# One tuned kernel, four edits: layer-norm scale as multiply then add, a first chunk without DMA transposes, reordered denominator matmuls, refitted planner constants

## The chip, the cores and the metric

The kernel runs on one NeuronCore of a Trainium2 chip. Time is device microseconds (us) of one execution. Kernels that are compared ran in turn on the same chip. A run has one number more, the granted clock: the mean share of full speed at which TensorE was allowed to run.

## The reference, cut to what matters

Two kinds of layer alternate, four layers in all, on x of 2048 positions by 512 features (bf16).

```python
def _A_ref(x, wqkv, wo):      # local: each position sees 8 positions, two apart; 32 heads of 16
    ...
    logits = jnp.where(mask[None, None, :, :], logits, -1e9)
    attn = _softmax(logits, axis=-1)
    ...
def _B_ref(x, wq, wk, wv, wo):    # full attention, 32 query heads, one shared key and value head
    ...
    p = _softmax(scores, axis=-1)
    ...
x = A_x
x = x + _A_ref(_layernorm(x, axis=-1), A_wqkv, A_wo)
x = x + _B_ref(_layernorm(x, axis=-1), B_wq, B_wk, B_wv, B_wo)
x = x + _A_ref(_layernorm(x, axis=-1), A_wqkv, A_wo)
x = x + _B_ref(_layernorm(x, axis=-1), B_wq, B_wk, B_wv, B_wo)
```

Full attention needs 32 x 2048 x 2048 exponentials per layer, twice. That is most of the work.

## The kernel before

The program is laid out by a **planner** in Python, when the kernel is built. Each operation has an estimated duration and a list of engines that may do it. The planner plays the run through in its own time and emits the instructions of every engine in the order of the played start times. Each engine is given this fixed order and waits at semaphores. An estimate that is off changes no result, but it can put an instruction that must wait ahead of one that could run.

The sequence is cut into four chunks of 512 positions. A chunk goes through layer norm, q/k/v, local attention, output, second layer norm, and the projections of full attention. A stream of tiles (128 keys by 512 queries) of full attention runs beside this, each tile's exponentials on ScalarE ("pt") or on VectorE with GpSimd ("t", "i"). The first pair of layers must have all four chunks before it can do most of its tiles.

```python
MM, SWITCH, DMA = 216.0, 90.0, 620.0                       # planned durations, ns
LAT = {"pe": 264.0, "act": 170.0, "dve": 135.0, "pool": 120.0, "sp": 2400.0}
BIAS = {"act": 0.0, "act2": 150.0, "vec": 120.0, "pv": 200.0, "copy": 0.0, "pass": 140.0}
...
def ln(self, src, deps, after=(0.0,) * 4):                 # layer norm of one chunk, four tiles
    ...                                                    # statistics on VectorE, power on GpSimd
    for i in range(4):
        def norm(op, i=i, xn=xn):
            self.chain(op.eng, self.pick(op).tensor_scalar(
                out=xn.t[:], in0=src(i), scalar1=mv[:, i, 0:1], scalar2=rstd[:, i:i + 1],
                op0=ALU.subtract, op1=ALU.mult))
        n = ... self.op({"dve": 690.0, "pool": 900.0}, 0, norm, [pw, *xn.prev], ...)
        tr = self.op("sp", 1250.0, ... nc.sync.dma_start_transpose(
                out=xnT[:, :, i * 128:(i + 1) * 128], in_=xn.t[:]) ...)
...
def split(op):                                             # K of a chunk into its masked layout
    for g in range(4):
        for h in range(2):
            r = slice(32 * g + 16 * h, 32 * g + 16 * h + 16)
            self.chain("sp", nc.sync.dma_start(out=self.k.t[r, :, :, h, :], in_=...))
...
ms = self.op("dve", 400.0, mask, [ex], ...)                # mask of the local probabilities
...
for j in range(2):                                         # denominators, by column half j
    ...
    runs = [(dj, pj[:, :, SPILL:NQ]), (dj[:, b0:4, 0:SPILL], pj[:, b0:4, 0:SPILL])]
    for out, rhs in runs:
        self.chain("pe", nc.tensor.matmul(out, lhsT=self.w.halves[:, gh, :], rhs=rhs, ...,
                                          tile_position=(0, 64 * j)))
```

## Time and profile before

| | kernel before |
|---|---|
| time | 1702.98 us, median of 3 (1702.31 to 1707.58) |
| span of the profiled run, granted clock | 1703.6 us, 0.916 |
| busy share: TensorE, VectorE, ScalarE, GpSimd | 92, 86, 83, 55% |
| first exponential of full attention | 87.7 us |

A busy share is an average over stages with different limits. The prediction below therefore reads it by stage. Lines of the profile name instructions by line, engine and tiles: `PE o L1289` is a matmul that writes tile `o`, issued by line 1289.

### The profile page before, as it was taken

Reading aid. Unit: us, or ns where it says so; the run is one execution under the profiler, and the core shown is the slowest. Engines: PE = TensorE matmul, PEld = TensorE weight load, DVE = VectorE, ACT = ScalarE, POOL = GpSimd, SP = SyncE. Lnnn points to the kernel's source line nnn. Section 1 sums busy time; section 2 is a strip of 40 time slices with the busy share of each in tenths; the row PEclk is TensorE's granted clock in tenths of the full one; section 3 lists DMA queues with packets and bytes.
Section 4 is the critical chain, followed back from the end, with each engine's and each line's share of the span. In section 5 each row is a group of like instructions: output and inputs, shape, how many; then the busy total and the mean of one; then the engine's idle time right before and its main releaser. Section 6 shows DMA issues by size and latency. Waiting matters only on the chain.

```text
span 1703.6 us, 41207 instructions
## 1 busy us (share of the span) xinstructions
PE 1559.3 (92%) x16604; PEld 522.1 (31%) x16643; DVE 1458.8 (86%) x2466; ACT 1416.0 (83%) x1718; POOL 943.0 (55%) x702
## 2 busy tenths in 40 slices
PE   3698989899999999999999999899999999999996
PEld 1343433422332224322342223322222222222221
DVE  2567685899789996899779997799999999999996
ACT  2375867698879987899878997699999999998994
POOL 4425354546465654666455663555666656565664
PEclk9577978799979997999979999799999999999997
DMA  5010101001100001000110001000100000000000
GB/s 149 15 26 14 27 11 29 6 14 37 31 21 12 11 22 26 14 14 12 22 23 17 12 18 26 3 17 4 38 24 12 12 24 11 13 13 23 12 18 14
DMA packets 101262, 36.02 MB, mean 21 GB/s; under 512 B 88840, under 2 KB 94600, under 8 KB 101064
## 3 DMA queue, kind: packets, MB, share of 16 engines
q1 hardware_dynamic: 100200, 31.48, 8.7%
q8 instruction: 132, 2.16, 0.5%
q10 hardware_dynamic: 864, 1.84, 0.3%
q14 instruction: 66, 0.54, 0.1%
HBM read 13.53 MB, written 2.61 MB: 9 GB/s over the span
## 4 chain that ended last, share of the span: by engine, by line
PE 38%; DVE 35%; ACT 15%; issue 8%; POOL 2%; DMA 1%; SPq 1%; DVEq 0%; ACTq 0%; POOLq 0%
DVE t L1268 24%; ACT pt L1264 14%; PE o L1289 12%; PE st L1249 8%; DVE i L1277 3%; PE y L992 3%; PE dv L1249 3%; PE oa L1171 2%; PE oa L1159 2%; PE q L992 2%; PE k L992 2%; PE qb L992 2%; DVE xn L1023 1%; PE v L1085 1%; PE st L1134 1%
## 5 line engine op out<-in xcount | busy, mean ns | idle before, releaser
L1264 ACT ACTIVATE pt<-st 128x1024 bf16<-128x1024 f32 x1306 | 1221.9, 1073 | 124.8 <-PE o L1289 55.4
L1273 POOL TENSOR_TENSOR i<-t,off 128x1024 int32<-128x1024 int32 x372 | 703.0, 1890 | 580.7 <-DVE i L1277 317.0
L1268 DVE TENSOR_SCALAR t<-dv 128x512 int16<-128x512 f32 x1485 | 931.7, 681 | 101.7 <-PE dv L1249 96.3
L1289 PE MATMUL o<-i,VEd 128*32 128x512 f16 x1470 | 280.8, 409 | 4.9 <-POOL i L1273 3.7
L1289 PE MATMUL o<-i,region 128*32 128x512 f16 x1500 | 277.2, 394 | 3.1 <-DVE i L1277 2.3
L1249 PE MATMUL dv<-QT,KAB 32*128 32x512 bf16 x735 | 264.0, 399 | 17.2 <-DVE t L1268 14.8
L1277 DVE TENSOR_SCALAR i<-t 128x2048 int16<-128x2048 int16 x372 | 267.0, 719 | 14.7 <-PE o L1289 6.3
L1249 PE MATMUL st<-QT,KAB 32*128 32x512 bf16 x1313 | 262.1, 400 | 15.4 <-ACT pt L1264 12.0
L1249 PE MATMUL dv<-QT,region 32*128 32x512 bf16 x750 | 262.0, 387 | 7.2 <-DVE t L1268 4.8
L1249 PE MATMUL st<-QT,region 32*128 32x512 bf16 x1298 | 255.1, 389 | 14.7 <-ACT pt L1264 11.4
L1289 PE MATMUL o<-pt,VEa 128*32 128x512 bf16 x1313 | 248.8, 413 | 2.5 <-DVE t L1268 0.6
L1289 PE MATMUL o<-pt,region 128*32 128x512 bf16 x1298 | 247.3, 397 | 0.0
L1289 PE MATMUL o<-t,VEd 128*32 128x512 f16 x735 | 195.2, 414 | 0.0
L1289 PE MATMUL o<-t,region 128*32 128x512 f16 x750 | 190.2, 394 | 1.0 <-DVE t L1268 1.0
L1249 PEld LDWEIGHTS <-KAB 32*128 32x128 bf16 x2048 | 87.0, 92 | 263.3 <-issue 256.4
L1249 PEld LDWEIGHTS <-region 32*128 32x128 bf16 x2048 | 84.1, 91 | 266.5 <-issue 262.2
L1289 PEld LDWEIGHTS <-region 128*32 128x32 f16 (+1 forms) x3548 | 82.1, 95 | 190.8 <-issue 179.1
L1289 PEld LDWEIGHTS <-VEd 128*32 128x32 f16 x2205 | 77.4, 96 | 129.0 <-issue 121.0
L1140 ACT ACTIVATE P<-st 128x576 bf16<-128x576 f32 (+1 forms) x128 | 80.3, 651 | 22.8 <-PE st L1134 22.1
L1146 DVE TENSOR_TENSOR P<-P,bandmask 128x288 int32<-128x288 int32 x128 | 71.2, 589 | 32.6 <-ACT P L1140 32.3
L1196 POOL TENSOR_TENSOR logs<-logs 128x256 f32<-128x256 f32 x64 | 41.9, 655 | 78.9 <-ACT rec L1187 78.8
L1289 PEld LDWEIGHTS <-VEa 128*32 128x32 bf16 x1313 | 57.6, 96 | 75.8 <-issue 70.8
(127 smaller groups left out, 1190.9 us busy)
## 6 DMA issues: line engine op xcount, KB each, us to landing
lb<-rd SPq DMA_DIRECT2D x31, 256.0 KB
k<-oncA SPq DMA_DIRECT2D x64, 64.0 KB
X<-X SPq DMA_DIRECT2D x124, 32.0 KB
w_sb<-in_A_wqkv_dram ACTq DMA_DIRECT2D x4, 384.0 KB
region<-in_A_x_dram SPq DMA_DIRECT2D x3, 512.0 KB
out_dram<-w_sb SPq DMA_DIRECT2D x3, 512.0 KB
xnT<-xn SPq DMA_TRANSPOSE x64
S<-X SPq DMA_DIRECT2D x62, 8.0 KB
```

The costliest lines, as they stand in the source:

```text
L992: self.chain("pe", self.nc.tensor.matmul(ps[:], lhsT=lhsT, rhs=rhs, start=(n == 0), stop=(n == len(pairs) - 1)))
L1140: ex = self.op("act", act_ns(2 * ncol), lambda op, P=P, sc=sc: self.chain("act", nc.scalar.activation(out=P.t[:, :, c0:UC], in_=self.st.po ...
L1146: self.chain(op.eng, self.pick(op).tensor_tensor(out=x, in0=x, in1=self.w.band[:].unsqueeze(1).to_broadcast([128, 8, NQ // 2]), op=ALU.bit ...
L1159: self.chain("pe", nc.tensor.matmul(o[32 * r:32 * r + 32, 0, q0:q0 + w], lhsT=vv[64 * a:64 * a + 64, j, 16 * gh:16 * gh + 32], rhs=P.t[64 ...
L1171: self.chain("pe", nc.tensor.matmul(out, lhsT=self.w.halves[:, gh, :], rhs=rhs, start=False, stop=False, skip_group_check=True, tile_posit ...
L1196: self.chain("pool", nc.gpsimd.tensor_tensor(out=lg.t[:], in0=lg.t[:], in1=lg.t[:], op=ALU.mult))
L1249: self.chain("pe", self.nc.tensor.matmul(out, lhsT=self.KAB[l][32 * g:32 * g + 32, a, kt * 128:(kt + 1) * 128], rhs=self.QT[32 * g:32 * g ...
L1264: self.chain("act", self.nc.scalar.activation(out=self.pt[pt][:, 0:n, :], in_=self.st.pop(key)[:, 0:n, :], func=AF.Exp, scale=E_SCALE))
L1268: self.chain("dve", self.nc.vector.tensor_scalar(out=self.t[buf][:, r, :].bitcast(I16), in0=self.dv[bank][:], scalar1=-U_BIAS, scalar2=U_B ...
L1273: i = self.nc.gpsimd.tensor_tensor(out=self.i[out][:, 0:n, :].bitcast(I32), in0=self.t[buf][:, 0:n, :].bitcast(I32), in1=self.w.off2[:, 0: ...
L1277: i = self.nc.vector.tensor_scalar(out=self.i[out][:, 0:n, :].bitcast(I16), in0=self.t[buf][:, 0:n, :].bitcast(I16), scalar1=J_OFF[j], sca ...
L1289: self.chain("pe", self.nc.tensor.matmul(self.o[bank][32 * g:32 * g + 32, :], lhsT=lhsT, rhs=rhs, start=first, stop=last, tile_position=(0 ...
```

## The change

Its intent: shorten the serial start (no DMA transposes, no DMA for K in the first chunk), let ScalarE take part of the layer norm, let the denominator matmuls of the two column halves overlap, and give the planner durations closer to the chip's.

```diff
-MM, SWITCH, DMA = 216.0, 90.0, 620.0
-LAT = {"pe": 264.0, "act": 170.0, "dve": 135.0, "pool": 120.0, "sp": 2400.0}
+MM, SWITCH, DMA = 216.0, 101.0, 620.0
+LAT = {"pe": 264.0, "act": 180.0, "dve": 142.0, "pool": 120.0, "sp": 2400.0}
... (evictions 41 and 19 ns shorter, exponentials 8 shorter, copies 605 -> 599, statistics 620 -> 596)
-    BIAS = {"act": 0.0, "act2": 150.0, "vec": 120.0, ...
+    BIAS = {"act": 0.0, "act2": 150.0, "vec": 180.0, ...
...
+        nm = ... nc.vector.scalar_tensor_tensor(out=nmr, in0=mv[:, :, 0], scalar=-1.0, in1=rstd,
+                                                op0=ALU.mult, op1=ALU.mult)
...
+                if op.eng == "act":
+                    k = nc.scalar.activation(out=xn.t[:], in_=src(i), func=AF.Identity,
+                                             scale=rstd[:, i:i + 1], bias=nmr[:, i:i + 1])
+                else:
+                    k = self.pick(op).tensor_scalar(..., scalar1=rstd[:, i:i + 1],
+                                                    scalar2=nmr[:, i:i + 1], op0=ALU.mult, op1=ALU.add)
...
+            if quick:                                       # chunk 0 of the first pair only
+                ... nc.tensor.transpose(out=pT[:, ft, :], in_=xn.t[:, ft * 128:(ft + 1) * 128], ...)
+                ... copy of pT into xnT on ScalarE or VectorE
...
+            if quick:
+                e0 = self.evac(m, self.k.t[:, t, :, 0, :], ..., self.w.kmask[:, 0:1])
+                e1 = self.evac(m, self.k.t[:, t, :, 1, :], ..., self.w.kmask[:, 1:2])
...
-            ms = self.op("dve", 400.0, mask, [ex], ...)
+            ms = self.op("dve", 500.0, mask, [ex], ...)
...
-                for j in range(2):          # both runs of half 0, then both of half 1
+                for q0, q1, b1 in ((SPILL, NQ, 0), (0, SPILL, b0)):
+                    for j in range(2):      # the wide run of both halves, then the narrow one
```

More of the change, by code (lines that the diff above doesn't have):

```diff
@@ L434, in act_ns @@
 def act_ns(cols, pointers=0):
-    return 93.0 + 0.833 * cols + 93.0 * pointers
+    return 52.0 + 0.833 * cols + 93.0 * pointers
 def dve_ns(cols):
-    return 85.0 + 1.04 * cols
+    return 66.0 + 1.04 * cols
 class Op:
@@ L583 @@
     GROUP = 4
-    BIAS = {"act": 0.0, "act2": 150.0, "vec": 120.0, "pv": 200.0, "copy": 0.0, "pass": 140.0}
+    BIAS = {"act": 0.0, "act2": 150.0, "vec": 180.0, "pv": 200.0, "copy": 0.0, "pass": 140.0}
     def __init__(self, sched, segments, ready, io):
@@ L688, in exp @@
         n = len(tiles)
-        t = 426.7 * n + 60
+        t = 426.7 * n + 52
         S.run("act", s, t)
@@ L709, in copy @@
         r, buf = len(self.filling), self.group_buf
-        done = s + 605 + LAT["dve"]
+        done = s + 599 + LAT["dve"]
         self.filling.append((tl, done))
-        S.run("dve", s, 605.0)
+        S.run("dve", s, 599.0)
         S.give(("bank", "vec"), bank, done)
@@ L716, in copy @@
         if len(self.filling) == self.GROUP:
-            self.flush(s + 605, None)
+            self.flush(s + 599, None)
     def flush(self, s, _):
@@ L730, in do_pass @@
         n = len(tiles)
-        t = 133.5 * n + 72 if e == "dve" else POOL_COL * 256 * n + 110
+        t = 134.0 * n + 70 if e == "dve" else POOL_COL * 256 * n + 110
         S.run(e, s, t)
@@ L995, in mm_full, with ln @@
         return self.op("pe", len(pairs) * MM, emit, deps, want=("bank", "aux"), solid=True, prio=self.PRIO, after=after)
-    def ln(self, src, deps, after=(0.0,) * 4):
+    def ln(self, src, deps, after=(0.0,) * 4, quick=False):
         nc = self.nc
@@ L1000, in ln @@
         stats, mv = sm.t[:, :, 0:6], sm.t[:, :, 6:8]
-        ve, rstd = (sm.t[:, :, n] for n in (8, 9))
+        ve, rstd, nmr = (sm.t[:, :, n] for n in (8, 9, 10))
         st = []
@@ L1005, in emit @@
                 self.chain("dve", nc.vector.bn_stats(out=stats[:, i, :], in_=src(i)))
-            st.append(sm.used(self.op("dve", 620.0, emit, [*deps[i], *sm.prev], prio=self.PRIO, after=after[i])))
+            st.append(sm.used(self.op("dve", 596.0, emit, [*deps[i], *sm.prev], prio=self.PRIO, after=after[i])))
         def aggr(op):
@@ L1016, in ln @@
             out=rstd, in0=ve, in1=self.w.nhalf[:], op=ALU.pow)), [ag], prio=self.PRIO))
+        nm = sm.used(self.op("dve", 250.0, lambda op: self.chain("dve", nc.vector.scalar_tensor_tensor(
+            out=nmr, in0=mv[:, :, 0], scalar=-1.0, in1=rstd, op0=ALU.mult, op1=ALU.mult)), [pw], prio=self.PRIO))
         self.xnT.renew()
@@ L1022, in norm @@
             def norm(op, i=i, xn=xn):
-                self.chain(op.eng, self.pick(op).tensor_scalar(
-                    out=xn.t[:], in0=src(i), scalar1=mv[:, i, 0:1], scalar2=rstd[:, i:i + 1], op0=ALU.subtract,
-                    op1=ALU.mult))
-            n = xn.used(sm.used(self.op({"dve": 690.0, "pool": 900.0}, 0, norm, [pw, *xn.prev], prio=self.PRIO,
-                                        port=("pool",))))
-            tr = self.op("sp", 1250.0, lambda op, i=i, xn=xn: self.chain("sp", nc.sync.dma_start_transpose(
-                out=xnT[:, :, i * 128:(i + 1) * 128], in_=xn.t[:])), [n, *self.xnT.prev], prio=self.PRIO)
@@ L1031, in ln @@
-            done.append(self.xnT.used(xn.used(tr)))
+                if op.eng == "act":
+                    k = nc.scalar.activation(out=xn.t[:], in_=src(i), func=AF.Identity, scale=rstd[:, i:i + 1],
+                                             bias=nmr[:, i:i + 1])
+                else:
+                    k = self.pick(op).tensor_scalar(out=xn.t[:], in0=src(i), scalar1=rstd[:, i:i + 1],
+                                                    scalar2=nmr[:, i:i + 1], op0=ALU.mult, op1=ALU.add)
@@ new lines, in norm, with turn @@
+                self.chain(op.eng, k)
+            n = xn.used(sm.used(self.op({"act": 830.0, "dve": 690.0, "pool": 940.0}, 0, norm, [nm, *xn.prev],
+                                        prio=self.PRIO, port=("pool",))))
+            cols = xnT[:, :, i * 128:(i + 1) * 128]
+            if quick:
+                def turn(op, xn=xn):
+                    pT = self.psum(op, [128, 4, 128], BF16, "pT")
+                    for ft in range(4):
+                        self.chain("pe", nc.tensor.transpose(out=pT[:, ft, :], in_=xn.t[:, ft * 128:(ft + 1) * 128],
+                                                             identity=self.w.ident[:]))
+                tr = xn.used(self.op("pe", 400.0, turn, [n, *self.xnT.prev], want=("bank", "aux"), solid=True,
+                                     prio=self.PRIO))
+                tr = self.op({"act": act_ns(512), "dve": 400.0}, 0, lambda op, cols=cols, tr=tr: self.chain(
+                    op.eng, (nc.scalar.copy if op.eng == "act" else nc.vector.tensor_copy)(
+                        out=cols, in_=self.y.pop(tr)[:])), [tr], frees=[tr], prio=self.PRIO)
+            else:
+                tr = xn.used(self.op("sp", 1300.0, lambda op, cols=cols, xn=xn: self.chain(
+                    "sp", nc.sync.dma_start_transpose(out=cols, in_=xn.t[:])), [n, *self.xnT.prev], prio=self.PRIO))
@@ L1032, in ln @@
+            done.append(self.xnT.used(tr))
         return done
@@ L1043, in chunk @@
         after = ((7300.0, 7300.0, 8800.0, 8800.0) if c == 0 else (9000.0 + 2500.0 * c,) * 4) if first else (0.0,) * 4
-        xops = self.ln(src, deps, after)
-        qkv = self.qkv(c, xops)
+        xops = self.ln(src, deps, after, l == 0 and c == 0)
+        qkv = self.qkv(c, xops, l == 0 and c == 0)
         units = [self.unit(c, t, kd, qkv) for kd in range(2) for t in range(4)]
@@ L1049, in chunk, with qkv @@
         return adds
-    def qkv(self, c, xops):
+    def qkv(self, c, xops, quick):
         nc, w_sb = self.nc, self.w.w_sb
@@ L1063, in qkv @@
             m = self.proj(lambda kt: w_sb[:, kt, D + t * 128:D + (t + 1) * 128], xops + self.oncA.prev, "k")
+            if quick:
+                view = lambda m=m: self.y[m][:].rearrange("p (b i) -> p b i", i=64)
+                e0 = self.evac(m, self.k.t[:, t, :, 0, :], view, 512, (), False, self.w.kmask[:, 0:1])
+                e1 = self.evac(m, self.k.t[:, t, :, 1, :], view, 512, [e0], True, self.w.kmask[:, 1:2])
+                kp.append([self.k.used(e0), self.k.used(e1)])
+                continue
             kp.append(self.oncA.used(self.evac(m, self.oncA.t[:, t, :], lambda m=m: self.y.pop(m)[:], 512)))
@@ L1072, in split @@
                         in_=self.oncA.t[r].rearrange("p t (b i) -> p t b i", i=64)))
-        k = [self.k.used(self.oncA.used(self.op("sp", 8 * DMA, split, [*kp, *self.k.prev], prio=self.PRIO)))] * 4
+        k = kp if quick else [[self.k.used(self.oncA.used(self.op("sp", 8 * DMA, split, [*kp, *self.k.prev],
+                                                                  prio=self.PRIO)))]] * 4
         vb = self.v.renew()
@@ L1100, in keep @@
                                                          in_=vb.t[:, 7, :, :, 2 * DH:VW]))
-            self.spill = self.op("pool", 1600.0, keep, [k[0], *v, *self.ks.prev, *self.vs.prev],
+            self.spill = self.op("pool", 1600.0, keep, [*k[0], *(k[3] if quick else ()), *v, *self.ks.prev, *self.vs.prev],
                                  port=("pool",))
@@ L1136, in score @@
                             stop=True, tile_position=(32 * g, 0), skip_group_check=True))
-            sc = self.op("pe", 300.0, score, [*qo[t], ko[t], *extra, *P.prev], want=("slot", "exp"),
+            sc = self.op("pe", 300.0, score, [*qo[t], *ko[t], *extra, *P.prev], want=("slot", "exp"),
                          solid=True, mode="row", prio=self.PRIO)
@@ L1147, in mask @@
                     out=x, in0=x, in1=self.w.band[:].unsqueeze(1).to_broadcast([128, 8, NQ // 2]), op=ALU.bitwise_and))
-            ms = self.op("dve", 400.0, mask, [ex], prio=self.PRIO, port=("dve",))
+            ms = self.op("dve", 500.0, mask, [ex], prio=self.PRIO, port=("dve",))
             def pv(op, gh=gh, P=P):
@@ L1163, in pv @@
                             begun.add(r)
-                for j in range(2):
-                    dj = o[64 * j:64 * j + 64, 1, :]
-                    dj = dj.rearrange("p (b q) -> p b q", q=64)
-                    pj = P.t[:, j, :].rearrange("p (b q) -> p b q", q=NQ)
-                    b0 = 0 if over else 1
-                    runs = [(dj, pj[:, :, SPILL:NQ]), (dj[:, b0:4, 0:SPILL], pj[:, b0:4, 0:SPILL])]
-                    for out, rhs in runs:
-                        self.chain("pe", nc.tensor.matmul(out, lhsT=self.w.halves[:, gh, :], rhs=rhs, start=False,
-                                                          stop=False, skip_group_check=True, tile_position=(0, 64 * j)))
+                b0 = 0 if over else 1
+                for q0, q1, b1 in ((SPILL, NQ, 0), (0, SPILL, b0)):
+                    for j in range(2):
+                        self.chain("pe", nc.tensor.matmul(
+                            o[64 * j:64 * j + 64, 1, :].rearrange("p (b q) -> p b q", q=64)[:, b1:4, 0:q1 - q0],
+                            lhsT=self.w.halves[:, gh, :],
+                            rhs=P.t[:, j, :].rearrange("p (b q) -> p b q", q=NQ)[:, b1:4, q0:q1],
+                            start=False, stop=False, skip_group_check=True, tile_position=(0, 64 * j)))
             kw = dict(want=("bank", "aux")) if gh == 0 else {}
-            m = self.op("pe", 310.0 + SWITCH + 190.0, pv, [ms, *vo, *extra, *pvs], solid=True, mode="c64",
+            m = self.op("pe", 340.0 + SWITCH + 150.0, pv, [ms, *vo, *extra, *pvs], solid=True, mode="c64",
                         prio=self.PRIO - 100.0, **kw)
@@ L1218, in b_in @@
         cs = slice(c * 512, (c + 1) * 512)
-        xops = self.ln(lambda i: self.x_sb[:, 4 * c + i, :], [[a] for a in adds])
+        xops = self.ln(lambda i: self.x_sb[:, 4 * c + i, :], [[a] for a in adds], quick=l == 0 and c == 0)
         done = []
@@ L1306, in evac @@
                        nc.vector.tensor_tensor(out=X.t[:], in0=X.t[:], in1=o[:], op=ALU.add))
-        e = X.used(self.op("dve", 605.0, evac, X.prev if fresh else list(X.cur), after=when, frees=[held], prio=-300.0))
+        e = X.used(self.op("dve", 599.0, evac, X.prev if fresh else list(X.cur), after=when, frees=[held], prio=-300.0))
         if self.parts_left[block]:
@@ L1377, in out_rows @@
                                          for t in range(4)], [self.ready[l, qc, t] for t in range(4)], "y"))
-        return self.op("dve", 605.0, lambda op: self.add_y(l, qc, qi, self.y.pop(m)[:]), [m], frees=[m], prio=-100.0)
+        return self.op("dve", 599.0, lambda op: self.add_y(l, qc, qi, self.y.pop(m)[:]), [m], frees=[m], prio=-100.0)
     def retire_w(self):
@@ L1437, in close_tail @@
         re = log.used(rec.used(self.op("act", act_ns(512), recip, [ln, *rec.prev])))
-        on = rec.used(self.op("dve", 605.0, scale, [re, self.retired]))
+        on = rec.used(self.op("dve", 599.0, scale, [re, self.retired]))
         rec.used(self.op("pool", 3000.0, see, [on, self.wiped]))
@@ L1465, in close_tail @@
             m = self.op("pe", MM, end, [on, begun[qi // 2]], solid=True)
-            self.op("dve", 605.0, lambda op, qi=qi: self.add_y(l, qc, qi, y[qi]), [m])
+            self.op("dve", 599.0, lambda op, qi=qi: self.add_y(l, qc, qi, y[qi]), [m])
     def run(self):
```

## The prediction

> **What bounds the kernel now.** I read the page's busy row and its 40 slices first, then busy time by stage, then the chain of waits over the first 120 us, then single groups of instructions.
>
> The slices say where the slack is. Nothing is full in the first two slices (0 to 85 us). In slices 3 to 8 (85 to 340 us) TensorE is full by the digits while VectorE and ScalarE hover between 5 and 8. From slice 9 to the last all three are close to full, and there the exponentials of the big attention, split between ScalarE and VectorE, are the work that counts.
>
> ```profile
> PE   3698989899999999999999999899999999999996
> DVE  2567685899789996899779997799999999999996
> ACT  2375867698879987899878997699999999998994
> PEclk9577978799979997999979999799999999999997
> ```
>
> By stage, over the last full-rate stretch (1107 to 1618 us, 511 us), the sums are PE 491, DVE 498, ACT 486: 96, 97 and 95%. No change of order can gain much there. The start is another matter. The columns are stretch, length, then busy us of PE, PEld, DVE, ACT, POOL, then the granted clock, DMA share and GB/s:
>
> ```profile
> 14.40:25.50 11.10, 0.00 (x0) 0.00 (x0) 4.25 (x12) 0.00 (x0) 5.32 (x4) 1.00 0.74 157
> 25.50:43.20 17.70, 13.17 (x110) 7.36 (x112) 0.46 (x1) 7.67 (x13) 0.00 (x0) 0.99 0.23 30
> 43.20:62.20 19.00, 17.51 (x433) 10.86 (x439) 10.38 (x22) 12.62 (x27) 8.99 (x15) 0.50 0.02 5
> 62.20:87.00 24.80, 11.64 (x115) 5.07 (x108) 12.27 (x31) 3.91 (x9) 8.47 (x8) 0.63 0.11 22
> ```
>
> Until 87 us there is one serial chain, the first chunk of 512 positions: layer norm, q/k/v, local attention, output, second layer norm, keys for the big attention. Only after it can the first exponential start (87.7 us). The chain of waits, in order of time (start, length, what):
>
> ```profile
> 13.37 1.06 POOL sm L1015
> 14.52 4.28 POOL xn L1023 x2
> 19.41 0.84 SPq L1029
> ...
> 22.96 2.45 DMA xnT<-xn
> 25.54 1.87 PE q L992 x4
> ...
> 34.43 0.59 ACT oncA L970
> ...
> 40.13 2.89 DMA k<-oncA
> ...
> 73.20 2.35 POOL xn L1023
> ...
> 78.18 2.43 DMA xnT<-xn
> 80.85 1.87 PE kb L992 x4
> ```
>
> The reader is to see three places where no engine computes: 14.5 to 25.5 (GpSimd scales two tiles, then four DMA transposes one behind the other), 34.4 to 43.2 (K through eight DMAs into its masked layout) and 73.2 to 80.9 (scale and transposes again). They are what the change aims at.
>
> **What the Trainium skill says.**
> (1) "GPSIMD Engine Reference", section 3.1, gives for 512 elements a best case of 769 ns. The trace disagrees for this operation: a subtract-and-multiply of 512 columns took 2276 ns (bf16 input) and 2505 ns (f32). No page says that multiply-then-add is quicker.
> (2) "ScalarE: Activation LUTs", section What ACT_TABLE_LOAD costs: each per-partition pointer operand adds about 93 ns. The trace agrees: a plain 512-column eviction is 586 ns, one with a scale pointer 691.
> (3) "TensorE: Matmul & The Clock Gate", Part 3, states that matmuls are "strict FIFO, no reordering". The trace disagrees, and one part of the change hangs on this (below).
> (4) The same page, Part 4: a 128x128 bf16 transpose takes about 390 ns alone and 275 ns in context, and does not count as activity for the clock. The kernel before has none, so no row can check it.
>
> **Part 1, first chunk by TensorE transposes, with the scale as multiply and add** (ScalarE can now take tiles; one small VectorE operation is added). First layer norm: before, from the end of the power at 14.42 to the first q matmul at 25.54, 11.1 us. After, worked out: the small operation 0.3 with its signal (the 128x4 L1012 takes about 0.17); scaling four tiles on three engines: ScalarE 586 + 2x100 = 0.8, VectorE two tiles in 1.1 as now, GpSimd 0.94 if the planner's new figure is true, so first tile at +0.8. Transposes: a cold 512-column matmul is spaced 1.87/4 = 0.47, so 128 columns 0.12 and a tile of four about 0.45; four tiles 1.8, plus about 0.2 of pipeline; the last copy 0.6; signals 0.2. Sum 0.3+0.8+1.8+0.2+0.6+0.2 = 3.9. **Gain 7.2.** If GpSimd still needs 2.2 us for its tile, the last transpose moves from +2.5 to about +2.6: almost nothing, as the tiles queue on TensorE anyway. Second layer norm: 73.11 to 80.85 is 7.7, the same sum gives 3.9, **gain 3.8.**
>
> **Part 2, masked copies of K in place of eight DMAs.** Now k is ready on TensorE at 34.4, v at 38.0 (34.33 + 3.68), but the bulk of local scores starts at 43.16. The new path adds four copies (two of 0.69 to 0.75 in place of one of 0.59 for each k): on ScalarE and VectorE 8x0.72 - 4x0.59 = 3.4 us, beside 12.5 us of projections during which VectorE has 0.46 us of work, so hidden. Scores can follow v at once. **Gain 43.2 - 38.0 = 5.2**, and about 1 more because the first scores can be exponentiated during v.
>
> **Part 3, denominators alternating column halves.** In program order the four matmuls are 256, 32 (half 0), 256, 32 (half 1). If the engine were strictly in order, half 1 would wait some 0.2 us for half 0, 128 times. But all rows of this line within 118.24 to 118.26 us, and then up to 118.50, are:
>
> ```profile
> L1171 PE MATMUL oa<-P,halves x2: 420/420/420, 118.2 to 118.2; 128*64 128x256 bf16 x2
> ...
> L1171 PE MATMUL oa<-P,halves x4: 234/327/420, 118.2 to 118.5; 128*64 128x256 bf16 x2, 128*64 128x32 bf16 x2
> ```
>
> Both wide ones start together and both narrow ones follow: the hardware already does what the new order asks for. Reading the start times of all 128 groups gives the same order, at 0, 7, 212 and 219 ns in the median. **Gain 0.**
>
> **Part 4, later chunks.** They keep DMA transposes and the DMA of K. Only the scale before the second layer norm's transposes is on their path: in chunk 1 the power ends at 162.28 and the first transpose starts at 164.62. VectorE's tiles take about 1.0 there beside GpSimd's 2.5. With 0.3 for the small operation and 0.8 to 1.0 on ScalarE or VectorE it starts near 163.7: **gain 0.9 x 3 = 2.7** for chunks 1 to 3 of the first pair of layers, where the chain holds back the stream (ScalarE waits up to 5.9 us there for matmuls). In the second pair the stream has work of its own and such latencies are hidden. Engine loads hardly move: of 64 scale tiles GpSimd has 20 and VectorE 44; perhaps 20 go to ScalarE, 0.8 each, 16 us more there and about 18 less on VectorE.
>
> **Part 5, the planner's constants.** They only decide the static order. The old figures are near the trace already: eight exponentials in a row took 7.44 us with a last one of 1.03, so 916 ns each; old 913, new 905. Six VectorE copies in 3.67 with a last one of 0.68 are 598 each; old 605, new 599. The one figure with a direction is the bias against VectorE tiles, 120 to 180, which moves tiles to ScalarE. In the last 511 us they stand at 97 against 95%; evening them out is worth half of (498-486)/511, about 1%, 5 us, at best. But every order after the first decision is dealt anew, which I take as noise of about 10 us either way; constants of this kind are kept when they helped, so I choose **gain 4**.
>
> **Sum.** 7.2 + 3.8 + 5.2 + 1 + 2.7 + 4 = 23.9. Does a shift of the first 87 us reach the end? Everything after waits for chunk 0's keys and VectorE and ScalarE had little before, so I count it whole. 1703 - 24 = 1679; I lean 2 us lower, to 1677, as the early stretch also gets a fuller TensorE and the clock there was only 0.50 to 0.63.
>
> **Rivals.**
> (a) The start's gain is handed back later: 85 to 340 us has one chunk after another, each about 86 us (second transposes start at 73.7, 164.6, 250.7, 338.0), with a half-clocked TensorE. If the stream, not the chunk chain, set that pace, an earlier start would only make a longer idle. Against it: VectorE waits 37 us there for score matmuls, with one wait of 11.3, so it runs dry and the chain sets the pace. If it happened: about 1692.
> (b) ScalarE becomes the bound through its new scale tiles and the bias: it has 4 to 5% slack in full stretches, 16 us plus moved tiles could eat it. Then the gain shrinks to 10 or so: 1692.
> (c) The new order is lucky or the alternation pays after all: 128 x 0.2 us is 26 us at most, half of it on a path. Against it, the start times above. It would make about 1660.
>
> **Range and chances.** The start is worth 16 to 20 with some confidence, the reshuffle has a spread of 10 or more and (a) to (c) some more. That gives 1677 with 1656 to 1694 for eight in ten. Two per cent faster is 1669 or less, about a third of the mass. Slower by 2% needs 1737, which nothing here suggests.
>
> **What would show it.** Right: first exponential near 70 us instead of 87.7; no transposes of chunk 0 on the DMA queue and eight fewer K transfers (56); GpSimd's scale tiles near 1 us; starts of the denominators still at 0, 7, 212, 219 ns; second transposes of chunks 1 to 3 about 17 to 20 us earlier than 164.6, 250.7, 338.0; the rest as long as before. Wrong: if chunk 3 ends no earlier although chunk 0 did (a); if ScalarE's idle goes and VectorE's grows (b); if pace after 340 us changes by over 1%, which is the planner, not the start.

## The result, and the profile after

The changed kernel takes **1650.73 us** (median of 4, 1649.93 to 1652.99) against 1705.01 for the kernel before in the same rounds. The ratio is **0.9684**, 95% interval 0.9663 to 0.9705. Ratios are the mean time of one kernel's fast runs over that of the other's of the same rounds, so they are not quite the ratio of the medians; in the experiments below the profiled round is left out of both means. The time lies below the predicted range (1656 to 1694): the direction was right, the size was about half of what came.

The chain of waits of the changed kernel, start, length, what:

```profile
13.34 1.06 POOL sm L1015
14.62 0.42 DVE xn L1029
15.09 0.62 PE pT L1040 x4
15.74 2.06 ACT xnT L1046 x4
17.84 1.86 PE q L992 x4
...
56.88 1.55 PE pT L1040 x12
...
59.36 1.89 PE kb L992 x4
```

The DMA transposes and the DMA of K are gone from the chain: from the end of the power to the first q matmul it is now 3.4 us where it was 11.1. The first exponential of full attention starts at 65.6 us.

Now the first chunk by stage. First the kernel before (its first two stages stand in the prediction: 14.4 to 25.5 and 25.5 to 43.2), then the changed one. The columns are stretch, length, busy us of PE, PEld, DVE, ACT and POOL, granted clock, DMA share, GB/s.

```profile
43.20:70.30 27.10, 23.00 (x500) 13.22 (x503) 14.55 (x30) 13.99 (x31) 12.03 (x19) 0.50 0.01 3
70.30:87.00 16.70, 6.15 (x36) 2.71 (x36) 8.09 (x24) 2.53 (x5) 5.43 (x3) 0.69 0.16 32
```

```profile
14.40:17.80 3.40, 1.89 (x16) 1.67 (x17) 3.34 (x7) 2.87 (x5) 0.90 (x1) 1.00 1.09 199
17.80:31.27 13.47, 13.43 (x96) 7.15 (x96) 4.08 (x12) 6.84 (x11) 1.63 (x2) 1.00 0.15 41
31.27:53.30 22.03, 17.77 (x514) 10.80 (x512) 16.49 (x31) 15.30 (x33) 12.10 (x18) 0.85 0.01 4
53.30:64.90 11.60, 7.51 (x51) 4.09 (x52) 7.03 (x23) 5.54 (x9) 4.90 (x5) 0.71 0.00 0
```

Layer norm 11.1 to 3.4, projections with K 17.7 to 13.5, local attention 27.1 to 22.0, second layer norm and keys 16.7 to 11.6. Four gains of 4 to 8 us, 22.1 in all. The third comes with a clock of 0.85 in place of 0.50.

Then the rest of the run, bounded by the moments when a chunk's last projection for full attention starts: chunks 1 and 2 of the first pair, the four chunks of the second pair, and what follows; before, then after.

```profile
87.00:180.30 93.30, 82.87 (x1021) 34.42 (x1021) 68.83 (x120) 62.93 (x94) 40.41 (x32) 0.78 0.11 19
180.30:267.30 87.00, 79.44 (x992) 33.01 (x992) 61.21 (x108) 64.32 (x94) 45.97 (x36) 0.80 0.11 20
...
351.10:1123.30 772.20, 730.99 (x7927) 245.91 (x7944) 681.13 (x1148) 670.66 (x817) 436.42 (x308) 0.93 0.09 19
1123.30:1703.60 580.30, 546.30 (x5044) 152.43 (x5044) 551.69 (x908) 533.35 (x579) 347.99 (x216) 0.97 0.06 16
```

```profile
64.90:149.90 85.00, 79.92 (x1042) 34.04 (x1039) 66.28 (x118) 65.41 (x97) 39.63 (x33) 0.84 0.12 20
149.90:232.20 82.30, 74.67 (x961) 31.49 (x958) 62.52 (x106) 61.61 (x93) 35.34 (x33) 0.85 0.12 21
...
314.70:1074.50 759.80, 727.17 (x7949) 246.61 (x7946) 670.83 (x1144) 674.91 (x828) 416.59 (x305) 0.93 0.09 19
1074.50:1647.30 572.80, 542.45 (x5039) 152.83 (x5035) 546.79 (x903) 534.96 (x583) 346.76 (x215) 0.98 0.06 16
```

The reader is to see that the gain did not stop at 65 us. Chunk 1 gives another 8.3, chunk 2 4.7, chunk 3 1.3 (83.8 to 82.5), the second pair 12.4, the rest 7.5. The predicted terms have 2.7 for chunks 1 to 3 and 4 for everything the planner does. So some 34 us stand where about 7 were expected, and the experiments had to find out whose the other 27 are.

### The profile page after: what moved, and what is told of

The parts are those of the page before. It is cut to its first block, busy times and chain, and to the rows that moved or that the text cites. A ratio compares the mean times of both kernels' runs of the same rounds, so it can differ in the third digit from the quotient of the medians.

```text
span 1647.3 us, 41270 instructions
## 1 busy us (share of the span) xinstructions
PE 1542.2 (94%) x16661; PEld 522.3 (32%) x16661; DVE 1444.9 (88%) x2458; ACT 1433.7 (87%) x1751; POOL 906.0 (55%) x697
## 4 chain that ended last, share of the span: by engine, by line
PE 42%; DVE 30%; ACT 17%; issue 8%; POOL 2%; DMA 0%; DVEq 0%; ACTq 0%; POOLq 0%
DVE t L1294 21%; ACT pt L1290 16%; PE o L1315 14%; PE st L1275 9%; PE dv L1275 3%; PE y L992 3%; DVE i L1303 3%; PE q L992 2%; PE k L992 2%; PE v L1112 2%; PE oa L1194 2%; PE oa L1186 2%; PE qb L992 2%; PE st L1161 1%; DVE P L1173 1%
## 5 line engine op out<-in xcount | busy, mean ns | idle before, releaser
L1290 ACT ACTIVATE pt<-st 128x1024 bf16<-128x1024 f32 x1309 | 1223.0, 1091 | 87.9 <-PE st L1275 36.8
L1315 PE MATMUL o<-i,VEd 128*32 128x512 f16 x1472 | 275.8, 408 | 4.9 <-POOL i L1299 2.5
L1315 PE MATMUL o<-i,region 128*32 128x512 f16 x1484 | 273.2, 389 | 3.2 <-POOL i L1299 2.2
L1275 PE MATMUL st<-QT,KAB 32*128 32x512 bf16 x1312 | 259.1, 402 | 14.9 <-ACT pt L1290 12.1
L1275 PE MATMUL dv<-QT,KAB 32*128 32x512 bf16 x736 | 257.9, 400 | 11.3 <-DVE t L1294 10.1
L1303 DVE TENSOR_SCALAR i<-t 128x2048 int16<-128x2048 int16 x370 | 258.0, 698 | 8.3
L1275 PE MATMUL st<-QT,region 32*128 32x512 bf16 x1306 | 253.8, 386 | 11.8 <-ACT pt L1290 9.1
L1275 PE MATMUL dv<-QT,region 32*128 32x512 bf16 x742 | 256.0, 384 | 5.4 <-DVE t L1294 4.0
L1315 PE MATMUL o<-pt,region 128*32 128x512 bf16 x1306 | 254.2, 391 | 0.0
L1315 PE MATMUL o<-t,VEd 128*32 128x512 f16 x736 | 189.2, 414 | 0.0
L1167 ACT ACTIVATE P<-st 128x576 bf16<-128x576 f32 (+1 forms) x128 | 78.8, 652 | 12.7 <-PE st L1161 11.6
L1222 POOL TENSOR_TENSOR logs<-logs 128x256 f32<-128x256 f32 x64 | 43.3, 676 | 71.8 <-ACT rec L1213 71.7
L1173 DVE TENSOR_TENSOR P<-P,bandmask 128x288 int32<-128x288 int32 x128 | 76.2, 632 | 7.1 <-ACT P L1167 6.2
L1315 PEld LDWEIGHTS <-VEa 128*32 128x32 bf16 x1312 | 57.7, 96 | 74.7 <-issue 70.6
```

The lines of the kernel that those rows point to most:

```text
L1167: ex = self.op("act", act_ns(2 * ncol), lambda op, P=P, sc=sc: self.chain("act", nc.scalar.activation(out=P.t[:, :, c0:UC], in_=self.st.po ...
L1173: self.chain(op.eng, self.pick(op).tensor_tensor(out=x, in0=x, in1=self.w.band[:].unsqueeze(1).to_broadcast([128, 8, NQ // 2]), op=ALU.bit ...
L1222: self.chain("pool", nc.gpsimd.tensor_tensor(out=lg.t[:], in0=lg.t[:], in1=lg.t[:], op=ALU.mult))
L1275: self.chain("pe", self.nc.tensor.matmul(out, lhsT=self.KAB[l][32 * g:32 * g + 32, a, kt * 128:(kt + 1) * 128], rhs=self.QT[32 * g:32 * g ...
L1290: self.chain("act", self.nc.scalar.activation(out=self.pt[pt][:, 0:n, :], in_=self.st.pop(key)[:, 0:n, :], func=AF.Exp, scale=E_SCALE))
L1303: i = self.nc.vector.tensor_scalar(out=self.i[out][:, 0:n, :].bitcast(I16), in0=self.t[buf][:, 0:n, :].bitcast(I16), scalar1=J_OFF[j], sca ...
```

## The experiments

Theory A: the first chunk's parts explain the start, and the planner's constants only deal a new order, good or bad by luck. Theory B: the constants (their fit, or the bias) are a cause of their own. Rivals for the rest: the layer norm's scale, and the denominators.

### One part alone, on the kernel before

**Constants and bias alone** (all the changed numbers, no other edit).

```diff
-MM, SWITCH, DMA = 216.0, 90.0, 620.0
+MM, SWITCH, DMA = 216.0, 101.0, 620.0
... (all other numbers of the change, and the bias 120 -> 180)
```

> The kernel before with the planner's refitted constants alone (no other part of the change). Theory A, the constants only deal a new static order: 1690 to 1715, within 1% of before either way. Theory B, a better fit is where the unexplained part of the gain (54 us measured, 17 of them in the first chunk) comes from: 1675 or less, with chunks 1 to 3 each some 5 us shorter.

1670.41 us, ratio 0.9832 (0.9766 to 0.9898). Numbers that leave every computation as it was take 29 us off. Chunk 1 is at 81.9 us, chunk 2 at 81.8. (The 17 us in the expectation are the predicted ones; the profiles have 22.1.)

**The scale alone.**

```diff
-    ... tensor_scalar(..., op0=ALU.subtract, op1=ALU.mult)           # VectorE or GpSimd
+    ... tensor_scalar(..., op0=ALU.mult, op1=ALU.add)                # or activation on ScalarE
```

> The kernel before with the layer norm's scale as multiply then add alone, ScalarE allowed, old constants and order rules. Theory A: GpSimd's tile falls from 2.3 to 2.5 us to about 0.8, the first layer norm gains about 3, each second layer norm 1 to 2: 1690 to 1697. Theory B, the scale is what shortened the later chunks: 1680 or less.

1689.97 us, ratio 0.9914 (0.9866 to 0.9962): at the edge of the span expected for theory A, with runs from 1684 to 1703. What was expected to bring it there is not in the profile, which is of the slowest run: from the end of the power to the first q matmul it takes 12.0 us where it was 11.1, and from the second power to the first matmul of the keys 7.5 for 7.7. The shorter stretches are chunks 1 and 2 (82.9 and 82.7 us for 93.3 and 87.0), in a new order. So the number was met without its mechanism.

**The first chunk by TensorE transposes and masked copies alone.**

```diff
-        xops = self.ln(src, deps, after)
-        qkv = self.qkv(c, xops)
+        xops = self.ln(src, deps, after, l == 0 and c == 0)
+        qkv = self.qkv(c, xops, l == 0 and c == 0)
... (the second layer norm likewise; old durations and old scale)
```

> The kernel before with the first chunk by TensorE transposes and masked K copies alone (old scale, old constants). All theories: the first chunk gains 12 to 15 us, as the GpSimd scale still takes two tiles. If a gain at the start is carried through whole: 1686 to 1693. If it grows on the way, because the stretch from 85 to 340 us runs with a different order: under 1680.

1684.51 us, ratio 0.9891 (0.9848 to 0.9934). The first exponential starts at 75.9 us, 11.8 earlier, and 19 us come out at the end; 8 of the difference are in chunk 1, again shorter (85.4 for 93.3). Instructions can be compared between two traces by line and tile name. By this, chunk 1 has a new order here, and everything after it has the order of the kernel before again (3 of 2270 VectorE instructions moved): 1525 us for 1523. So here too the gain of the start is kept.

**The order of the denominators alone.** The planner's cost of this block is untouched, so the two programs differ in nothing but 128 swaps.

```diff
-                for j in range(2):
-                    for out, rhs in runs: ...
+                for q0, q1, b1 in ((SPILL, NQ, 0), (0, SPILL, b0)):
+                    for j in range(2): ...
```

> The kernel before with nothing but the order of the four denominator matmuls changed; the planner's order of everything else is the same instruction for instruction. Theory A, the hardware already starts both halves together: within 2 us of before, and start times 0, 4 to 7, 212, 219 ns as before. Theory B, in-order issue makes half 1 wait 0.2 us in each of 128 groups: 10 to 26 us faster, and the starts differ from before.

1700.92 us, ratio 1.0002 (0.9944 to 1.006). **No gain.** The median starts are 0, 3, 212, 218 ns for 0, 7, 212, 219. (The second wide matmul followed the first by 6 or 7 ns in every group before, by 3 or 4 here, so the two programs are not the same on the chip.) In the changed kernel the line within 0.3 us of one group reads as it did before:

```profile
L1194 PE MATMUL oa<-P,halves x4: 224/324/422, 38.8 to 39.0; 128*64 128x256 bf16 x2, 128*64 128x24 bf16 x2
```

So theory B has the lead, and theory A fails in its size. But one thing speaks for luck: chunk 1 took 93.3 us in the kernel before, and fell to 82 to 85 in every one of three quite different edits. Was the kernel before just dealt a bad order there?

### Bias, durations, and changes that mean nothing, on the kernel before

> The kernel before with the bias against VectorE tiles alone at 180 for 120. Theory B1, the bias is what the refit gained by (29 us in all, alone on before): 1670 to 1680, with more tiles on ScalarE than before's 2611. Theory B2, it was the fitted durations: 1695 to 1708. Theory L, any new order does as well, as before's own order is an unlucky one in chunk 1 (93 us, where every other order run so far took 82 to 85): 1690 or so, chunk 1 at 82 to 86 us.

```diff
-    BIAS = {..., "vec": 120.0, ...
+    BIAS = {..., "vec": 180.0, ...
```

1669.94 us, ratio 0.9797 (0.9759 to 0.9836). Yet hardly a tile changed engines: ScalarE's instructions for them rose from 1306 to 1314, VectorE's fell from 1485 to 1468. The balance of the engines can hardly be what gained; a later run, with the bias old in the changed kernel, says so more strongly.

> The kernel before with the refitted durations and latencies alone, bias left at 120. Theory B2, the fit is what counts: 1670 to 1680. Theory B1, the bias: 1695 to 1708. Theory L, a new deal of the order: chunk 1 at 82 to 86 us and some 1690.

(The same numbers as in the first run, bias left at 120.) 1679.56 us, ratio 0.9836 (0.98 to 0.9872). Alone, bias and durations give 35 and 28 us, together 29: they are not two sums to be added, they are three orders.

> The kernel before with a change that means nothing: the planner takes TensorE's latency as 265 ns for 264. It deals a new order (some tenth of the instructions move). Theory L, luck of the order: it moves the time by up to 10 us, and chunk 1 falls from 93 to 82 to 86 us. Theory F, the fit or the bias made the gain: within 4 us of before.

```diff
-LAT = {"pe": 264.0, ...
+LAT = {"pe": 265.0, ...
```

1687.97 us, ratio 0.9878 (0.9836 to 0.992). **A nanosecond that means nothing took off 1.2%.** Theory F ("within 4 us") fell, and the 10 us of theory L were too few.

> A second change that means nothing on the kernel before: the planner takes a VectorE pass 1 ns longer. Theory L: up to 10 us from before either way, chunk 1 near 82 to 86 us unless it starts with the same order. Theory F: within 4 us of before. With the run above it gives the size of the luck in a new order.

```diff
-        t = 133.5 * n + 72 if e == "dve" else ...
+        t = 133.5 * n + 73 if e == "dve" else ...
```

1699.67 us, ratio 0.9961 (0.9919 to 1.0003). Chunk 1 here is 91.2 us. So of three orders dealt with the old constants (this one, the one above and the kernel before's), the kernel before's is the slowest, and they spread over 1.2%.

The traces answer the question about chunk 1. This second nudge leaves the order of all engines as it was until about 360 us, so it did not deal chunk 1 anew. Four profiles have the kernel before's order in chunk 1, but for a few instructions: its own, the denominators', this one, and the changed kernel with all old constants (below). Their chunk 1 takes 90.0 to 93.3 us, 91.3 in the mean. In the fifteen others that keep the DMA there it takes 79.8 to 88.8, 84.4 in the mean. So the kernel before did have a bad order in chunk 1, worth some 7 us.

### One part taken out of the changed kernel

**All constants old, bias too; everything else as changed.**

> The changed kernel with all of the planner's old constants, bias included. Theory A, the first chunk's shortening (22 us in the profile) is a gain of its own and the constants a second one: 1671 to 1682, first exponential near 66 us, the later chunks as long as before. Theory L, all is luck of the order: anything from 1650 to 1690, with no pattern by stage.

1672.06 us, ratio 0.9818 (0.9781 to 0.9855). The first chunk ends at 69.9 us here, 17.1 earlier than in the kernel before. So the refit is worth 0.9818 - 0.9684, 1.3% or 23 us, on top of the others, and 5 of these in the first chunk. By the two profiles it is 28 us: 5 in the first chunk, 6 in chunk 1 (90.8 for 85.0, the bad order), 3 less in chunks 2 and 3, and 20 after the first pair of layers.

**The old scale.**

> The changed kernel with the old scale (subtract, multiply, on VectorE or GpSimd only). If the scale is worth what its rows show (GpSimd 2.3 to 2.5 us a tile against 0.8 to 0.9): first exponential 4 to 6 us later, second layer norms 1 to 2 us longer, 1655 to 1664. If it is worth nothing beyond: 1651.

1657.68 us, ratio 0.9727 (0.9687 to 0.9767). The first exponential is 6.1 us later (71.7) and the whole about 7. The scale's rows by tile, kernel before and changed kernel, count, then busy us and mean ns:

```profile
L1023 POOL TENSOR_SCALAR xn<-x_sb,sm 128x512 bf16<-128x512 f32 x15 | 37.5, 2505 | 0.3
```

```profile
L1029 POOL TENSOR_SCALAR xn<-x_sb,sm 128x512 bf16<-128x512 f32 x11 | 9.7, 884 | 3.1 <-DVE sm L1017 2.4
```

GpSimd does multiply-and-add almost three times as fast as subtract-and-multiply (2362 ns in this run, the changed kernel with the old scale).

**DMA transposes and DMA copies in the first chunk.**

> The changed kernel with the first chunk by DMA transposes and DMA copies of K as before. If the first chunk's gain reaches the end whole: first exponential near 82 us and the whole 14 to 18 us longer, 1664 to 1669. If it is handed back later: within 5 us of the changed kernel, 1651 to 1656.

1667.87 us, ratio 0.9798 (0.9759 to 0.9837), 17 us more. This pair is the cleanest of all, as after the first chunk VectorE, ScalarE and GpSimd have the same instructions in the same order, by line and tile name: the last two stages of this kernel are

```profile
328.70:1089.30 760.60, 725.70 (x7929) 246.56 (x7945) 671.34 (x1144) 675.15 (x828) 417.20 (x305) 0.93 0.09 19
1089.30:1663.60 574.30, 544.62 (x5034) 152.21 (x5034) 546.27 (x903) 535.90 (x583) 347.18 (x215) 0.97 0.06 16
```

with 1144, 828 and 305, then 903, 583 and 215 instructions on VectorE, ScalarE and GpSimd, as in the changed kernel above, and lengths within 2 us of it. The start is 18.6 us longer (83.5 for 64.9), the span 16.3: in chunks 1 to 3, 4.6 us are handed back (245.2 for 249.8), and 2.3 come in the last two stages. **Most of what the first chunk gains reaches the end.**

**A change that means nothing, on the changed kernel.**

> The changed kernel with a change that means nothing: the planner takes VectorE's latency 1 ns longer. Luck in the changed kernel's own order would show as a loss: if its constants were kept for a lucky order, 1655 to 1670; if the fit is good by itself, within 5 us of 1651.

```diff
-LAT = {"pe": 264.0, "act": 180.0, "dve": 142.0, ...
+LAT = {"pe": 264.0, "act": 180.0, "dve": 143.0, ...
```

1652.34 us, ratio 0.9717 (0.9677 to 0.9757): no loss. But this nudge dealt only a part anew. VectorE's instructions keep the changed kernel's order until 1374 us and TensorE's until about 728, so it says little about the order of the first 700 us.

### Which part of the refit, and what paces the first pair

Those 12 runs put the missing 20-odd us into the refit. The next six ask which part, and by what.

> The changed kernel with the bias back at 120, refitted durations kept. If the bias is what the refit gained by: 1665 to 1672, as without the whole refit. If the durations are: 1649 to 1655. If they overlap, as on the kernel before (34 and 28 alone, 29 together): 1653 to 1662.

```diff
-    BIAS = {..., "vec": 180.0, ...        (changed kernel)
+    BIAS = {..., "vec": 120.0, ...
```

1652.75 us, ratio 0.9684 (0.9648 to 0.9721). The bias is worth nothing here, though alone on the kernel before it had seemed worth 35 us. Nor is the balance: ScalarE has 1302 of these instructions and VectorE 1492, where the changed kernel has 1309 and 1478, at the same ratio. And since the order is a new one from 67 us on, this run says what the nudge could not: the changed kernel does not depend on its one order.

> The changed kernel with the old durations, bias kept at 180. If the bias is what counts: 1649 to 1656. If the durations are: 1665 to 1672. If they overlap: 1653 to 1662.

(All durations old, bias 180.) 1670.26 us, ratio 0.9801 (0.9765 to 0.9838). It differs from the changed kernel in local attention of the first chunk. The timeline of this kernel (start, length in us, engine, line, what it does, in brackets the idle time before it and what ended that) has a matmul group that TensorE sat idle before:

```profile
36.64 0.94 PE L1161 MATMUL st<-q,k 32*128 32x72 bf16 x16 [1.24 <-ACT P L1167]
```

The stretch from 45 to 54 us of the same kernel (columns: the stretch, its length, busy us and count of each engine, TensorE first, then the granted clock, the DMA share and GB/s):

```profile
45.00:54.00 9.00, 7.87 (x178) 4.38 (x178) 5.00 (x11) 3.60 (x8) 2.63 (x4) 0.50 0.01 4
```

The same stretch of the changed kernel:

```profile
45.00:54.00 9.00, 5.88 (x192) 3.51 (x180) 7.19 (x14) 4.56 (x10) 4.33 (x6) 1.00 0.02 5
```

With the old durations TensorE sat 1.24 us before a matmul that waited for ScalarE to free its buffer, the clock had dropped to half, and it did 178 matmuls in 7.87 busy us; with the new ones 192 in 5.88 at full clock. Its first chunk ends at 70.6 us for 64.9. The changed kernel has a wait of the same kind (0.95 us at 32.56), and between 28 and 65 us all its waits for ScalarE and VectorE to finish with the probabilities sum to 2.4 us for 3.8 here. The clock differs more: from the first score to the end of the second power it is at half for 25.8 of 31.1 us here, for 8.6 of 24.8 in the changed kernel. That the waits brought the clock down is not shown.

> The kernel before with one planned duration changed, the mask's 400 ns to 500 (its rows show a mean of 589). Theory M, this too short figure put matmuls that wait for a mask ahead of others in TensorE's order: 1680 to 1688 with chunks 0 to 3 shorter by 3 to 5 us each. Theory L, only a new deal: within what two meaningless changes gave, 1680 to 1704, with no pattern by chunk.

```diff
-            ms = self.op("dve", 400.0, mask, [ex], ...)      (kernel before)
+            ms = self.op("dve", 500.0, mask, [ex], ...)
```

1686.87 us, ratio 0.99 (0.9852 to 0.9949). Chunks 0 to 3 take 87.9, 79.8, 81.9 and 91.8 us, for 87.0, 93.3, 87.0 and 83.8: no pattern by chunk, and a time that the meaningless nanosecond reached too. Theory M is not shown by it.

> The changed kernel with the old durations except the mask's, which is at the new 500. Theory M, the mask's figure is the part that counts: 1650 to 1657. If the rest of the refit counts: 1664 to 1674.

(The changed kernel with old durations, the mask's at 500.) 1653.42 us, ratio 0.9726 (0.9663 to 0.979). This would settle it for the mask, were it not for the next run.

> The changed kernel with the old durations and a change that means nothing (TensorE's latency 265 for 264). If the fit is the cause: 1664 to 1676, near the 1670 and 1672 of the two kernels with old durations. If those two were unlucky orders: under 1660.

(The changed kernel with old durations, TensorE's latency 265 for 264.) 1657.93 us, ratio 0.9718 (0.9681 to 0.9755). It means nothing and gains as much as the mask's figure. So the part of luck is real in the changed kernel as well, after the first chunk, which ends at 71.6 us. By ratio, the three orders with old durations stand at 0.9818, 0.9801 and 0.9718, and the three with new ones at 0.9684, 0.9684 and 0.9717. The means differ by 0.8%, some 14 us, but the ranges touch, and the nudged order with new durations shares its first 700 us with the changed kernel's. **That new durations are better for the whole run is likely, not settled; that the mask's figure is the one that counts stays open.**

In the first chunk it is more than likely. Each of the four combinations of first-chunk edit and scale was run with both sets of durations, and with the new ones the chunk ends earlier every time: 64.9 for 69.9 us with both, 71.1 for 75.3 with the old scale, 83.5 for 88.9 with the DMAs, 83.5 for 87.0 with neither. The bias went along in these pairs, but alone it left the chunk at 87.6 for 87.0 and at 64.9 for 64.7, and the nudge of the changed kernel left it at 64.8. For the rest of the run the profiles show a pattern that was seen only afterwards and that no run tested. After the first chunk, the seven kernels with old bias and all old durations take 1597 to 1617 us, the eleven with bias, durations or both new 1575 to 1597 (the mask's figure alone, 1593, and the last kernel below are left out). If it holds, either refit brings most of that gain, which would fit 35 and 28 us alone and 29 together.

> The changed kernel with TensorE transposes and masked K copies in chunks 1 to 3 of the first pair of layers as well. If the chain of chunks paces that stretch: each of the three chunks 5 to 12 us shorter (82 to 85 now), 1620 to 1640. If the stream's work paces it: chunks as long as before and 1648 to 1660, as the masked copies add work to ScalarE and VectorE.

```diff
-        xops = self.ln(src, deps, after, l == 0 and c == 0)
+        xops = self.ln(src, deps, after, l == 0)
-        qkv = self.qkv(c, xops, l == 0 and c == 0)
+        qkv = self.qkv(c, xops, l == 0)
... (the second layer norm likewise; the masked copies wait for the last readers of K)
```

1636.16 us, ratio **0.9605** (0.957 to 0.964): **this version beats both kernels**, the changed one by some 14 us. The stages show why it is 14 and not 50. ScalarE's exponentials of full attention (first busy column PE, then ACT), chunks 1 to 3 and the stage after, changed kernel first:

```profile
64.90:314.70 249.80, 36.17 (x222) 113.55 (x118) 0.85 0.12 21
314.70:482.80 168.10, 47.05 (x256) 116.80 (x124) 0.92 0.12 24
```

```profile
63.70:262.40 198.70, 18.81 (x122) 67.09 (x68) 0.85 0.01 2
262.40:468.50 206.10, 60.16 (x352) 161.23 (x173) 0.97 0.09 20
```

The three chunks are 51 us shorter, so the chain of chunks does pace that stretch. But in the shorter time ScalarE did 68 exponentials instead of 118, and the next stage pays for them: 38 us longer, with 173 for 124. In chunk 0 there is no such work to miss, and most of a microsecond saved there is kept.

## Why the prediction was wrong, point by point

- **Part 1, first layer norm, "Gain 7.2".** Right: 11.1 to 3.4 us (7.7). ScalarE's copies came one after the other in 2.06 us, the transposes in 1.89 for 16, against 1.8 estimated. The record of one transpose is 312 ns long in the mean, between the two figures that the prediction quotes from the skill.
- **Part 1, second layer norm, "gain 3.8".** From the end of the power to the first matmul of the keys 7.7 became 3.3 us, a gain of 4.4; the whole stage went from 16.7 to 11.6.
- **Part 2, masked copies, "Gain 43.2 - 38.0 = 5.2".** 17.7 to 13.5, so 4.2: TensorE was busy for 13.43 of the 13.47 us, so the copies were hidden as argued, but the projections took more than the 12.5 assumed (12.1 in the nudged kernel, in the same order). The 1 us more did not come: the first score starts at 31.27, after the last v matmul at 31.07.
- **Sum for the first chunk: 7.2 + 3.8 + 5.2 + 1 = 17.2.** With the old constants it is 17.1 (69.9 for 87.0). That it is so close is partly luck: a kernel with the order unchanged (the denominators') ended this chunk 1.4 us from the kernel before. In the changed kernel it is 22.1; the other 5 go with the new durations, in local attention, for which the prediction had no term.
- **"I count it whole".** Right: 18.6 at the start, 16.3 at the end in the pair with equal counts. Rival (a), gains handed back, is refuted for most of chunk 0's gain. (Its "half-clocked TensorE" overstates the trace: chunks 1 and 2 had a clock of 0.78 and 0.80.) It is half true for chunks 1 to 3, as the last experiment shows.
- **Part 3, denominators, "Gain 0".** Right, ratio 1.0002.
- **Part 4, "gain 0.9 x 3 = 2.7".** Wrong by its own step, "0.3 for the small operation". From the end of the power to the first transpose, chunks 1 to 3 took 2.3, 1.3 and 3.2 us before, and 3.1, 4.6 and 2.9 after. The small 128x4 operation took 1.5 us in the median and 0.16 at the least. All nine long ones (1.47 to 1.85 us) lie over a pass on GpSimd and end 22 to 27 ns after it; none of the seven short ones does. In chunk 2 of the changed kernel, VectorE's operation and GpSimd's pass:

```profile
215.36 1.54 DVE L1017 SCALAR_TENSOR_TENSOR sm<-sm 128x4 f32<-128x4 f32 x1
```

```profile
214.99 1.89 POOL L1299 TENSOR_TENSOR i<-t,off 128x1024 int32<-128x1024 int32 x1 [1.43 <-PE o L1315]
```

  They end together, at 216.90 and 216.88. (In this chunk another 1.8 us passed between the power and the start of the small operation.) The Trainium skill says it in "GPSIMD Engine Reference", section 1, Specifications: GpSimd shares SBUF interfaces with VectorE, with contention for VectorE instructions that have two SBUF inputs. The prediction read the page and did not use this.
- **Part 5, the planner's constants, "gain 4".** **This is the step that failed.** Its reasons were that single figures hardly moved, and that evening out two engines is worth 5 us at best (a sum for the last 511 us only; over all 1360 us after 340 the same 1% would be about 14). The runs show that balance is not it (the bias moved 8 more instructions to ScalarE, and the changed kernel is as fast with it undone), and that the order itself is worth far more than "noise of about 10 us either way": a nanosecond moved the kernel before by 20 us, and the refit gave 23 on top of the other parts. The prediction took the kernel before as a typical order; it is the slowest of the three dealt with its constants, with some 7 us lost in chunk 1. Of the 23, about 5 go with the durations in the first chunk. How much of the rest is a better fit and how much a bad order left behind was not settled. The prediction's own sign came up: "if pace after 340 us changes by over 1%, which is the planner". From the end of chunk 3 on it fell from 1352.5 to 1332.6 us, 1.5%.
- **Rival (c), "lucky order", 1660.** Nearest to what happened, but put down in half to the denominators.
- **The lean for the clock, 2 us.** Too small. In the 35 runs of the kernel before, time falls by 0.89 us for each 0.001 of granted clock (correlation -0.87). The changed kernel's profiled run has 0.933 for 0.916: by that slope some 15 of the 54 us (an estimate) go with the clock. Whether a better order lifts the clock or the clock makes the order look better, these runs do not separate.

## What to carry to other kernels

A saving in a stretch where nothing else can run was kept nearly whole at the end (16.3 of 18.6 us); a saving in a stretch where deferred work fills the gaps was worth only what that work did not cost later (14 of 51). When a kernel's order is dealt by a planner, measure what a meaningless nudge does before crediting any edit that re-deals it, look in the trace from where on the nudge changed the order, and give an edit's effect from pairs with the same order where they can be had. Read start times before believing that instructions run in the order written.

## What the Trainium skill lacked or had wrong

- "TensorE: Matmul & The Clock Gate", Part 3, has matmuls in strict order. In this trace all 128 groups written as 256, 32, 256, 32 columns on two column halves (24 for 32 in a quarter of them) start at 0, 7, 212 and 219 ns in the median, with both wide ones first, and writing them in that order changes the time by a ratio of 1.0002. That the engine and not a step of the build puts them so is not shown by itself; that the gap of 7 ns became 3 with the new order speaks for the engine.
- "GPSIMD Engine Reference", section 3.1, does not say that the pair of operations matters: 512 f32 columns took 2505 ns as subtract-multiply and 884 ns as multiply-add.
- "ScalarE: Activation LUTs", section What ACT_TABLE_LOAD costs: about 93 ns for each pointer operand. Here, for 512 columns from PSUM, 586 ns with none and 685 to 691 with one, so 99 to 105. (The scale's 811 with two reads SBUF and is no clean pair with these.)
- No page says how far a run's time follows the granted clock in a kernel with all engines busy: 0.89 us per 0.001 in 35 runs of 1704 us.
